# Moving the sums of w_out and the storing of its tiles in a fused retention and feed-forward kernel

## The chip, the cores and the metric

The kernel runs on one core of one Trainium2 chip. The metric is the device time of one execution in microseconds (us); the time of a kernel is the median of its runs.

## What is computed

Eight batches, eight heads, 576 positions, head dimension 64: retention (attention without softmax, with a decay per head), then a feed-forward layer of 512 -> 2048 -> 512 with g = h - tanh(h).

```python
scores = scale * np.matmul(q, k.transpose(0, 1, 3, 2))
ret = scores * Dmat[None]                    # Dmat: gamma_h ** (i - j) for i >= j, else 0
attn = np.matmul(ret, v)
x = attn.transpose(0, 2, 1, 3).reshape(4608, 512)
h = x @ w_in                                 # 512 x 2048
g = h - np.tanh(h)
out = g @ w_out                              # 2048 x 512
```

## The kernel before

**Work and its order.** The 576 positions are cut into nine chunks n = 0 to 8 of 64 positions, so a chunk holds 512 tokens (8 batches x 64). The 2048 hidden features are cut into sixteen F tiles f of 128. Each matmul operand in float32 is held as two words, high ("hi", `gh`, `xh`) and low ("lo", `gl`, `xl`), and a product is made of high x high, high x low and low x high. The program order is kept on each engine (`in_order`); a DMA may further be put behind a named instruction (`behind`). Nearly all DMAs go through one queue, that of SyncE (SP), in the order in which they stand in the program: a DMA that waits for its data holds all behind it.

**Chunks 0 and 1** come first. **Chunk 2** is then done in two halves. In the first, the loop over f calls `mm1(2, f)` (h of one F tile, tanh on ScalarE (ACT) at L533, the difference on VectorE (DVE) at L534, a store to DRAM) and, on VectorE, two pieces of the sums of w_in (`summed`). In the second, `stage_b(2, 0)`, the F tiles run in pairs: at an even f `attend(m)` makes one *turn* of the retention for later chunks (a turn is two batches of one chunk: scores, outputs, state), and each f has `mm2(2, f)`, twelve matmuls into the output's four PSUM banks. Here `split` makes the two words of g two tiles ahead (ACT copy, then VectorE), `fetch` loads g four tiles ahead, and `load_turn` loads q and k (t = 0) or v and k (t = 1) of later turns. The load of v for turn m+2 is put behind the seventh matmul of the odd F tile's `mm2`. `scale_v` (L301), four ACT instructions, multiplies v of a turn with its table, one turn ahead, inside `attend`. The fifth and sixth matmul of the odd tile's `mm2` wait for the loads of q of turn m+2 and of v of turn m+1.

**Keeping w_out.** The last six chunks use a scheme with seven products for a pair of 2 x 2 blocks in place of eight, for which sums of the weight blocks are needed. `keep_whole` adds the two words of one F tile of w_out on VectorE (L1021) and stores the result to `owhole` in DRAM (L1022). Before the change it does so for tiles 0 to 7 at the odd f of the first half, into the buffers with tag "cv" (four, which the activations of `mm1` also use), and for tiles 8 to 15 at the odd f of the second half, into two quarters of `work`.

**Chunks 3 to 8** are taken in pairs: `stage_c(na, ...)` for na = 3, 5 and 7. Each has eight *steps* p, one for a pair of F tiles. A step (for na = 3 and 5) begins with a stretch of the retention for a later turn (`attend_c`: 64 x 64 matmuls at L344, which include those that read the scaled v), and then has seven products `product_c` numbered 0 to 6, six matmuls each (L1078). Between them stand the VectorE sums `u2` (L1202), `u4` (L1210), `c22` (L1218), `c12` (L1225), `g11` (L1241), `c21` (L1247); ACT's tanh (L1183); GpSimd's (POOL's) difference for `c22`, `c12` and `c21` (L1187); and four spills to DRAM through SP (L1140), each two products after it was made. In odd steps VectorE also makes the four sums `sums_of` (L1117 to L1120). `prep_turn(m0 + p + 1, 1)` after product 5 is the scaling of v (L301) that the next step's stretch needs.

**The sums of w_out** are spread over the sixteen steps of na = 3 and 5, numbered `step_` 0 to 15, two for each pair j of F tiles: `load_whole(j)` (L1027) loads two tiles from `owhole` to `work`, `out_sums` makes four VectorE subtractions of 128 x 256 (L1035), `out_words` is one ACT copy to the high words (L1040), `out_lows` one VectorE subtraction for the low words (L1044), and `store_sums` stores to `osum` and `ovar` (L1048, L1049). The next load goes to the buffer that the store reads. Before the change, the even step has `out_sums` after product 4, `out_words` after the tanh of product 5 and ahead of the scaling of v, `out_lows` after product 6; the odd step has `store_sums` after product 0 and the next `load_whole` after product 4. `load_raws` and `load_sums` (L1062, L1070) load the weights' words for the products, the latter two steps ahead.

After na = 7, whose steps have no retention, a last part (`second_product`, L1399 and L1403) makes the second layer of chunks 3 to 8 with seven products in the same way.

Of the kernel before, what the change touches and what calls it, by code (L numbers as in the profile page):

```python
# [9 lines left out]
F32 = mybir.dt.float32  # L10
# [82 lines left out]
def retention_ffn(ctx: ExitStack, tc: tile.TileContext, ins, out, spill, wvar, owhole, osum, ovar):  # L93
# [924 lines left out]
    def keep_whole(f, r):  # L1018

        w = wout[f].bitcast(F32)  # L1020
        nc.vector.tensor_tensor(r, w[:, 0], w[:, 1], op=ALU.add)  # L1021
        nc.sync.dma_start(owhole[:, f], r)  # L1022

    def load_whole(j):

        if j < NPAIR:
            nc.sync.dma_start(work[:, 0:2], owhole[:, 2 * j : 2 * j + 2])  # L1027
# [18 lines left out]
    def store_sums(j):  # L1046

        nc.sync.dma_start(osum[:, :, j], work[:, 3].rearrange("p (v m) -> p v m", v=2))  # L1048
        nc.sync.dma_start(ovar[:, :, j], work[:, 0:2])  # L1049
# [94 lines left out]
    def stage_c(na, m0, lows):  # L1144

        nb, last_ = na + 1, na + 2 == NC
        if not last_:
            first_sources(na)
        for p in range(NPAIR):
            if p == 1 and not last_:  # L1150
                new_sources(na)
            back = (na - LATE) // 2 % 2 == 1
            j = NPAIR - 1 - p if back else p
            homes_ = (("o0", "own")[p % 2], "new", "h", "h") if last_ else (("o0", "h")[p % 2], "o1", "o2", "o3")
            step_ = None if last_ else NPAIR * (na - LATE) // 2 + p
            sums_of = None if last_ else attend_c(m0 + p)
            if sums_of and p == NPAIR - 1:
                sums_of()
                sums_of = None
            u2, u4 = [pool.tile([P, BLK], F32, tag=t, name=f"u{t}{na}_{j}") for t in ("gh", "gl")]  # L1160
            x, y, z, v = [
                psp.tile([P, BLK], F32, tag=t, bufs=2 if t == "h" else 1, name=f"p{w}{na}_{j}")
                for w, t in zip("xyzv", homes_)
            ]
            f1, f2 = 2 * j, 2 * j + 1
            c22, c12 = [pool.tile([P, BLK], F32, tag="g", bufs=3, name=f"c{t}_{na}_{j}") for t in (22, 12)]
            c21 = pool.tile([P, BLK], F32, tag="gl", name=f"c21_{na}_{j}")

            def done(k):
                made_at[0] += 1  # L1170
                if last_:
                    ahead_c(p, k)
                elif p == NPAIR - 1 and k < 6:
                    lows.insert(0 if k == 5 else len(lows), renew(na, k))
                spill_made(2)

            def low():
                if lows:
                    lows.pop(0)()

            def tanh(c):
                th = pool.tile([P, BLK], F32, tag="cv", bufs=4, name=f"th{na}_{j}")
                nc.scalar.activation(th, c, AF.Tanh)  # L1183
                return th

            def away(n, c, f):
                nc.gpsimd.tensor_tensor(c, c, tanh(c), op=ALU.subtract)  # L1187
                to_spill.append((made_at[0], n, f, c))

            product_c(na, j, 0, x)  # L1190
            nc.scalar.copy(u2, x)
            if na > LATE and p == 0:
                lows.append(renew(na - 2, 6))
            done(0)
            if not last_:
                load_turn(m0 + p + 3, 0)
            if step_ == 0:
                load_whole(0)
            if step_ is not None and step_ % 2:
                store_sums(step_ // 2)  # L1200
            product_c(na, j, 1, y)
            nc.vector.tensor_tensor(u2, y, u2, op=ALU.add)  # L1202
            low()
            done(1)
            if not last_:
                load_turn(m0 + p + 2, 1)
                if na == LATE:
                    load_raws(6 + p)
            product_c(na, j, 2, z)
            nc.vector.tensor_tensor(u4, z, u2, op=ALU.add)  # L1210
            if not last_:
                prep_turn(m0 + p + 2, 0)
            if sums_of:
                sums_of()
            low()
            done(2)
            product_c(na, j, 3, v)
            nc.vector.tensor_tensor(c22, v, u4, op=ALU.add)  # L1218
            low()
            done(3)  # L1220
            y = psp.tile([P, BLK], F32, tag=homes_[1], bufs=1, name=f"pw{na}_{j}")
            product_c(na, j, 4, y)
            load_sums(na, j - 2 if back else j + 2)
            away(nb, c22, f2)
            nc.vector.tensor_tensor(c12, y, u4, op=ALU.add)  # L1225
            done(4)
            if tables and not last_:
                load_tables(tables.pop())
                set_tables()
            if step_ is not None and step_ % 2:  # L1230
                load_whole(step_ // 2 + 1)
            if step_ is not None and step_ % 2 == 0:
                words = out_sums(step_ // 2)
            product_c(na, j, 5, x, False)
            if not last_ and p == NPAIR - 1:
                low()
            away(nb, c12, f1)
            g11 = tanh(x)
            if step_ is not None and step_ % 2 == 0:
                out_words(words)  # L1240
            nc.vector.tensor_tensor(g11, x, g11, op=ALU.subtract)  # L1241
            to_spill.append((made_at[0], na, f1, g11))
            if not last_:
                prep_turn(m0 + p + 1, 1)
            done(5)
            product_c(na, j, 6, v, False)
            nc.vector.tensor_tensor(c21, v, u2, op=ALU.add)  # L1247
            away(na, c21, f2)
            low()
            if step_ is not None and step_ % 2 == 0:  # L1250
                out_lows(words)
            done(6)
        spill_made(0)

# [186 lines left out]
    def fetch_on(n, f):  # L1441
        if f < NF:
            fetch(n, f)

    def stage_b(n, m0):

        fetch(n, 3)
        for f in range(NF):
            def ahead():
                if f + 2 < NF:  # L1450
                    split(n, f + 2, fetched.pop((n, f + 2)), f % 3 == 0)

            if n == 2 and f == 1:
                load_tables(FIRST)
            m, odd = m0 + f // 2, f % 2 == 1
            if n < NC - 1 and not odd:
                attend(m, ahead)
            else:
                ahead()
            if n == NC - 1:  # L1460
                fetch_on(n, f + 4)
            if n == LATE - 1:
                if odd:
                    keep_whole(8 + f // 2, work[:, f // 2 % 2])
                if f in (11, 13):
                    load_sums(LATE, (f - 11) // 2)
                if f > 3 and f % 2 == 0:
                    load_raws(f // 2 - 2)
            if (n, f) != (NC - 1, NF - 2):
                seen = [came.get((m + 2, 0)), came.get((m + 1, 1))] if n < NC - 1 and odd else []  # L1470
                names = mm2(n, f, [a for a in seen if a])
            if n < NC - 1:
                if n != LATE - 3 or (m + 3 - odd, odd) not in ((held, True), (held + 1, True)):
                    load_turn(m + 3 - odd, int(odd), names[6 if odd else 2])
                fetch_on(n, f + 4)
            if odd and tables:
                load_tables(tables.pop())
                set_tables()
            if n == 2 and f == 2:
                set_tables()  # L1480


    for f in range(NF):
        mm1(2, f, seen=[here[24, 1], came[1, 0]] if f == NF - 1 else [])
        if f == 0:
            mm2(*late[-1])
        if f == 1:
            follow(1)
        for _ in range(2):
            next(summed, None)  # L1490
        if f == 2:
            load_turn(2, 0)
        if f == 6:
            prep_turn(2, 0)
            load_turn(1, 0)
            load_turn(1, 1)
        if f in (9, 10):
            prep_turn(1, f - 9)
        if 10 < f < 14:
            fetch(2, f - 11)  # L1500
        if f > 13:
            split(2, f - 14, fetched.pop((2, f - 14)), False)
        if f % 2:
            keep_whole(f // 2, pool.tile([P, DM], F32, tag="cv", bufs=4, name=f"whole{f // 2}"))
    assert next(summed, 0) == 0
    work = pool.tile([P, 4, DM], F32, tag="xl1", bufs=1, name="work")
    stage_b(2, 0)
    lows = []
    for n in range(LATE, NC, 2):
        stage_c(n, 8 * (n - FIRST) // 2 + 8 if n < NC - 2 else None, lows)  # L1510
# [84 lines left out]
```

## Time and profile before

| | |
|---|---|
| Time, median of 3 runs | 886.43 us (886.01 to 888.31) |
| The profiled execution: time, span | 883.95 us, 882.1 us |
| TensorE matmul (PE) | 835.8 us busy, 95% |
| VectorE (DVE) | 642.0 us, 73% |
| ScalarE (ACT) | 425.7 us, 48% |
| GpSimd (POOL) | 109.7 us, 12% |
| DMA | 207.27 MB, mean 235 GB/s |

The span is the time from the first to the last instruction of the profiled execution; the time stands 1.85 us above it. PE is TensorE's matmul row, PEld its weight loads, which overlap with it, SP the DMA queue. In a table of stretches the columns are: length, busy time and number of instructions for PE, PEld, DVE, ACT and POOL, the clock that TensorE was granted (1.00 is full), the busy share of the 16 DMA engines, and GB/s. In a list of waits the columns are the engine and line that stood idle, what it waited for, the total in us, how many times, and the longest. In a timeline they are start and duration in us, engine, line, operation, and in brackets the engine's idle time before it and what ended it. In a line's own view durations are in ns, minimum/median/maximum.

### The profile page before, as it was taken

What the parts mean: (1) busy time and instruction counts of PE and PEld (TensorE: products, weight loads), DVE (VectorE), ACT (ScalarE), POOL (GpSimd) and SP (SyncE); (2) the same over time, 40 slices, a digit from 0 to 9 for tenths busy, and PEclk for the clock granted to TensorE, in tenths of its full rate; (3) what the DMA queues carried; (4) which work ended last, traced back from release to release, by engine and by line L of the source; (5) the groups of instructions that cost most, each with busy time, mean ns of one, the idle gap of its engine ahead of it and who ended that gap; (6) DMA issues with size and microseconds to landing.
All of it is one profiled execution on the core that took longest, in us unless ns stands there. A gap on an engine that the chain in (4) does not pass through costs nothing. (4 is left out here: it accounts for less than half of the span.)

```text
span 882.1 us, 19386 instructions
## 1 busy us (share of the span) xinstructions
PE 835.8 (95%) x7893; PEld 696.5 (79%) x7894; DVE 642.0 (73%) x950; ACT 425.7 (48%) x767; POOL 109.7 (12%) x87
## 2 busy tenths in 40 slices
PE   8999999999998986999888999999999999999997
PEld 6788888878877765877776777888788888888886
DVE  6998877776776745566694556756789888888884
ACT  4987755443343433242453243643555544445442
POOL 0000101020000001231332132343320000000000
PEclk9999999999999989999998899999999999999999
DMA  9968968884887878998677685489795445444311
GB/s 344 362 220 291 329 221 253 258 281 138 270 318 264 273 283 273 334 308 312 233 256 256 214 285 184 144 315 322 272 388 169 132 140 153 126 140 147 120 25 48
DMA packets 101768, 207.27 MB, mean 235 GB/s; under 512 B 9136, under 2 KB 42288, under 8 KB 99120
## 3 DMA queue, kind: packets, MB, share of 16 engines
q1 hardware_dynamic: 101232, 205.25, 68.5%
q8 instruction: 62, 1.02, 0.5%
q10 hardware_dynamic: 448, 0.79, 0.2%
q14 instruction: 26, 0.21, 0.1%
HBM read 134.17 MB, written 71.83 MB: 234 GB/s over the span
## 5 line engine op out<-in xcount | busy, mean ns | idle before, releaser
L1399 PE MATMUL b<-w,s 128*128 128x512 f32 x504 | 176.1, 397 | 1.0 <-ACT u L1413 0.7
L1187 POOL TENSOR_TENSOR c<-c,th 128x512 f32<-128x512 f32 x72 | 97.0, 1353 | 335.5 <-ACT th L1183 286.2
L1403 PE MATMUL b<-w,s 128*128 128x256 f32 x504 | 130.6, 280 | 0.0
L1399 PEld LDWEIGHTS b<-w,s 128*128 128x128 f32 x504 | 91.8, 188 | 18.8 <-ACT u L1413 1.0
L1183 ACT ACTIVATE th<-c 128x512 f32<-128x512 f32 x72 | 45.1, 630 | 117.4 <-DVE c L1218 92.0
L1403 PEld LDWEIGHTS b<-w,s 128*128 128x128 f32 x504 | 95.2, 189 | 5.5
L514 PE MATMUL h<-xh,wi 128*128 128x512 f32 x380 | 97.0, 392 | 1.6 <-DVE g L534 0.9
L572 PE MATMUL o<-wo,gh 128*128 128x512 f32 x344 | 89.7, 397 | 6.8 <-DMA vr<-in_qkv_dram 5.9
L344 PE MATMUL own<-qk,vr 64*64 64x64 f32 x888 | 64.2, 242 | 22.4 <-ACT vr L301 19.9
L514 PEld LDWEIGHTS h<-xh,wi 128*128 128x128 f32 x380 | 70.6, 188 | 17.0 <-DVE g L534 1.3
L572 PEld LDWEIGHTS o<-wo,gh 128*128 128x128 f32 x344 | 63.7, 189 | 23.0 <-DMA vr<-in_qkv_dram 7.2
L344 PEld LDWEIGHTS own<-qk,vr 64*64 64x64 f32 x888 | 50.2, 151 | 23.7 <-ACT vr L301 21.2
L1078 PE MATMUL px<-xhv,raw 128*128 128x512 f32 x192 | 65.0, 422 | 0.0
L344 PE MATMUL own<-qk,state 64*64 64x64 f32 x888 | 63.9, 238 | 0.0
L1202 DVE TENSOR_TENSOR ugh<-py,ugh 128x512 f32<-128x512 f32 x24 | 16.6, 692 | 53.9 <-PE py L1078 48.1
L514 PE MATMUL h<-xl,wi 128*128 128x512 f32 x192 | 51.8, 390 | 0.0
L572 PE MATMUL o<-wo,gl 128*128 128x512 f32 x172 | 48.5, 396 | 1.2 <-DMA vr<-in_qkv_dram 1.2
L344 PEld LDWEIGHTS own<-qk,state 64*64 64x64 f32 x888 | 49.6, 150 | 0.0
L1413 ACT COPY u<-b 128x512 f32<-128x512 f32 x36 | 21.1, 586 | 52.4 <-PE b L1399 52.4
L1362 DVE TENSOR_TENSOR s<-sums,s 128x1024 fp32r<-128x1024 f32 x36 | 43.8, 1232 | 2.1 <-ACT s L1358 2.1
L1358 ACT CAST s<-sums 128x1024 fp32r<-128x1024 f32 x36 | 37.9, 1053 | 13.1 <-DVE sums L1360 9.7
L1078 PEld LDWEIGHTS px<-xhv,raw 128*128 128x128 f32 x192 | 37.0, 201 | 8.2
(317 smaller groups left out, 1882.9 us busy)
## 6 DMA issues: line engine op xcount, KB each, us to landing
wt<-wvar_dram SPq DMA_DIRECT2D x20, 1024.0 KB, 5.4
spill_dram<-c SPq DMA_DIRECT2D x72, 256.0 KB, 4.4
qk<-in_qkv_dram SPq DMA_DIRECT2D x29, 512.0 KB, 5.6
vr<-in_qkv_dram SPq DMA_DIRECT2D x29, 512.0 KB, 5.9
ge<-spill_dram SPq DMA_DIRECT2D x12, 1024.0 KB, 5.8
go<-spill_dram SPq DMA_DIRECT2D x12, 1024.0 KB, 5.1
s<-spill_dram SPq DMA_DIRECT2D x46, 256.0 KB, 4.2
spill_dram<-g SPq DMA_DIRECT2D x36, 256.0 KB, 3.7
```

The source lines that it names most:

```text
L344: nc.tensor.matmul(out_, w, x, start=start, stop=stop)
L514: nc.tensor.matmul(hp, win[f][:, cc // 2, a, cc % 2 * P : (cc % 2 + 1) * P], x[:, cc, :], start=(k == 0), stop=(k == 3 * NCC - 1))
L572: nc.tensor.matmul(ops[n][t], g[:, t * P : (t + 1) * P], wout[f_][:, a, :], start=(f_ == first and k == 0), stop=(f_ == final and k == 2),)
L1078: nc.tensor.matmul(into, w[:, a, k], x[:, k], start=start and i == 0, stop=i == len(terms) - 1, skip_group_check=not start,)
L1183: nc.scalar.activation(th, c, AF.Tanh)
L1187: nc.gpsimd.tensor_tensor(c, c, tanh(c), op=ALU.subtract)
L1202: nc.vector.tensor_tensor(u2, y, u2, op=ALU.add)
L1358: nc.scalar.copy(hi, src)
L1362: nc.vector.tensor_tensor(lo, src, hi.bitcast(F32), op=ALU.subtract)
L1399: nc.tensor.matmul(to, hi[:, j], ws, start=fresh and j == 0, stop=last_, skip_group_check=not fresh)
L1403: nc.tensor.matmul(to[:, 0], lo[:, j], ws[:, 0], start=False, stop=False, skip_group_check=not fresh)
L1413: nc.scalar.copy(t, to)
```

## The change

In the first half of chunk 2 the sums of tiles 0 to 7 go to the buffers "gh" and "gl" in turn, at f = 1, 3, 5, 7, 9, 11, 12 and 13. The store of a kept tile is issued by a new function, `store_whole`, in the next F tile, behind that tile's own loads; in the second half the sum itself stands after `mm2` and the loads. In the steps, `out_sums` moves from after product 4 of the even step to its end; `out_words` and `out_lows` move to the odd step, after products 2 and 3; `store_sums` moves from after product 0 to after product 5 of the odd step; and `load_whole` from after product 4 of the odd step to after product 1 of the next even step. No arithmetic is added or left out.

```diff
@@ keep_whole
         w = wout[f].bitcast(F32)
         nc.vector.tensor_tensor(r, w[:, 0], w[:, 1], op=ALU.add)
-        nc.sync.dma_start(owhole[:, f], r)
+        to_keep.append((f, r))
+
+    to_keep = []
+
+    def store_whole():
+
+        while to_keep:
+            f, r = to_keep.pop()
+            nc.sync.dma_start(owhole[:, f], r)
@@ stage_c, a step
             done(0)
             if not last_:
                 load_turn(m0 + p + 3, 0)
-            if step_ == 0:
-                load_whole(0)
-            if step_ is not None and step_ % 2:
-                store_sums(step_ // 2)
             product_c(na, j, 1, y)
...
                 if na == LATE:
                     load_raws(6 + p)
+                if step_ % 2 == 0:
+                    load_whole(step_ // 2)
             product_c(na, j, 2, z)
...
             done(2)
+            if step_ is not None and step_ % 2:
+                out_words(words)
             product_c(na, j, 3, v)
             nc.vector.tensor_tensor(c22, v, u4, op=ALU.add)
             low()
+            if step_ is not None and step_ % 2:
+                out_lows(words)
             done(3)
...
-            if step_ is not None and step_ % 2:
-                load_whole(step_ // 2 + 1)
-            if step_ is not None and step_ % 2 == 0:
-                words = out_sums(step_ // 2)
             product_c(na, j, 5, x, False)
...
             g11 = tanh(x)
-            if step_ is not None and step_ % 2 == 0:
-                out_words(words)
             nc.vector.tensor_tensor(g11, x, g11, op=ALU.subtract)
...
             done(5)
+            if step_ is not None and step_ % 2:
+                store_sums(step_ // 2)
             product_c(na, j, 6, v, False)
...
             low()
             if step_ is not None and step_ % 2 == 0:
-                out_lows(words)
+                words = out_sums(step_ // 2)
             done(6)
@@ stage_b
             if n == LATE - 1:
-                if odd:
-                    keep_whole(8 + f // 2, work[:, f // 2 % 2])
...
                 fetch_on(n, f + 4)
+                store_whole()
+                if odd:
+                    keep_whole(8 + f // 2, work[:, f // 2 % 2])
@@ first half of chunk 2
+    KEEP = (1, 3, 5, 7, 9, 11, 12, 13)
...
-        if f % 2:
-            keep_whole(f // 2, pool.tile([P, DM], F32, tag="cv", bufs=4, name=f"whole{f // 2}"))
+        store_whole()
+        if f in KEEP:
+            at = KEEP.index(f)
+            keep_whole(at, pool.tile([P, DM], F32, tag=("gh", "gl")[at % 2], name=f"whole{at}"))
...
     stage_b(2, 0)
+    store_whole()
```

## The prediction

> **What bounds the kernel now.** I read the page, the busy time by stretch, the waits, then the timeline of single steps. First the three stretches that the change touches: the last fifteen F tiles' first products of chunk 2 with their sums, chunk 2's second half (eight pairs of F tiles), and the sixteen steps with `step_` 0 to 15. Columns: length, busy us by engine, granted clock, DMA share, GB/s.
>
> ```profile
> 217.25:259.35 42.10, 41.20 (x182) 33.54 (x180) 30.62 (x55) 13.98 (x27) 0.00 (x0) 1.00 0.84 287
> 259.35:333.73 74.38, 65.92 (x1218) 52.66 (x1217) 44.83 (x91) 31.20 (x81) 0.00 (x0) 0.95 0.79 281
> 333.73:563.10 229.37, 203.93 (x2560) 168.76 (x2560) 145.05 (x233) 91.20 (x196) 60.42 (x46) 0.93 0.74 256
> ```
>
> TensorE (PE, first number) is the bound, but idle for 0.90, 8.46 and 25.44 us here, and below full clock in the last two. The waits of PE, ACT and the DMA queue (SP), which follow, say for whom.
>
> ```profile
> PE own L344 <- ACT vr L301: 19.9, 9, 5.5
> PE o L572 <- DMA vr<-in_qkv_dram: 8.5, 6, 3.4
> ```
> ```profile
> ACT work L1040 <- DVE work L1035: 19.7, 8, 5.6
> ACT vr L301 <- DMA vr<-in_qkv_dram: 19.3, 7, 5.8
> ```
> ```profile
> SPq L1022 <- DVE work L1021: 42.4, 8, 7.1
> ```
>
> So PE waits nine times for ACT's scaling of v (`scale_v`, L301), which stands behind `out_words` (L1040), which waits for `out_sums` (L1035) on VectorE; and six times for a load of v that SP issues late, since SP is held for 42.4 of 74 us by the store in `keep_whole` (L1022).
>
> **Chunk 2's second half.** SP around the worst pair, and ACT at the landing:
>
> ```profile
> 312.97 0.32 SPq L1022 DMA_DIRECT2D owhole_dram<-work  x1
> 313.35 1.06 SPq L1070 DMA_DIRECT2D wt<-wvar_dram  x1
> 314.50 0.38 SPq L895 DMA_DIRECT2D vr<-in_qkv_dram  x1
> ```
> ```profile
> 320.12 1.28 ACT L301 ACTIVATE vr<-vr,vtab 128x128 f32<-128x128 f32 x4 [5.75 <-DMA vr<-in_qkv_dram]
> ```
>
> It is a ring: the load of v for turn m+2 stands behind the store of w_out's words on SP; that store waits for VectorE's sum, which in VectorE's order follows `split`'s low words; these wait for ACT's copy, which follows the scaling of v of turn m+1, which waits for its own load. Each load thus starts only after the one before has landed and been worked on. The change stores a tile after the next F tile's loads, so its sum is done and SP isn't held. What then holds the load of v is its own wait for the seventh matmul of the odd F tile (`late`), which leaves five matmuls of the pair to run, and PE needs it a pair later. A pair costs
>
> ```profile
> 285.41:293.10 7.69, 7.69 (x154) 6.39 (x153) 6.06 (x13) 4.16 (x12) 0.00 (x0) 1.00 0.83 277
> 310.53:323.42 12.89, 9.46 (x153) 7.22 (x152) 5.48 (x12) 4.01 (x11) 0.00 (x0) 0.83 0.85 317
> ```
>
> 7.69 us where nothing is late. 8 x 7.69 = 61.5, so at most 12.9 us go. In the pairs of F tiles 11 and 13 the 1 MB load of L1070 still stands just ahead of the load of v (1.06 us of issue), for which I leave 0.8 each, an estimate between 0 and 1.5: **-11.3**. VectorE's order of the sums is unchanged (only the last moves behind two output copies). The eight stores are as many as before, each landing beside PE's work.
>
> **The first stretch.** Sums now write buffers of their own ("gh", "gl") instead of the four "cv" buffers that the activations use.
>
> ```profile
> ACT g L533 <- DMA owhole_dram<-whole: 4.3, 1, 4.3
> ```
>
> ACT stood 4.3 us for such a buffer; PE's idle 0.90 us is the end of that. Three sums now fall in F tiles 11 to 13, one per tile, 0.7 us more on a VectorE that is busy 30.6 of 42.1: covered. **-0.9** (0 to -0.9).
>
> **The steps.** Steps 0, 1, 2, 3 by PE's starts (even, odd, even, odd), then steps 6, 8 and 10:
>
> ```profile
> 333.73:345.50 11.77, 11.77 (x172) 9.77 (x171) 7.63 (x14) 4.28 (x9) 2.47 (x2) 1.00 0.67 182
> 345.50:365.43 19.93, 14.45 (x172) 12.04 (x171) 9.54 (x19) 5.44 (x13) 2.56 (x3) 0.83 0.98 343
> 365.43:377.44 12.01, 12.01 (x172) 9.99 (x171) 7.73 (x11) 4.67 (x11) 5.00 (x5) 1.00 0.94 333
> 377.44:393.09 15.65, 13.76 (x172) 11.44 (x171) 9.22 (x18) 5.43 (x13) 2.69 (x3) 0.89 0.88 296
> 420.65:433.93 13.28, 12.18 (x172) 9.99 (x171) 7.74 (x11) 4.67 (x11) 5.02 (x5) 1.00 0.76 269
> 448.08:461.33 13.25, 12.28 (x172) 10.13 (x171) 12.16 (x17) 7.66 (x15) 5.26 (x4) 1.00 0.64 224
> 477.81:494.11 16.30, 13.90 (x171) 11.31 (x170) 8.18 (x13) 4.68 (x11) 5.00 (x5) 0.90 0.66 227
> ```
>
> The same work takes 12.0 us in an even step and 15.65 in the odd one. The end of step 2, on VectorE, ACT and PE:
>
> ```profile
> 375.49 3.28 DVE L1035 TENSOR_TENSOR work<-work 128x256 f32<-128x256 f32 x4
> ```
> ```profile
> 376.25 0.60 ACT L1183 ACTIVATE th<-px 128x512 f32<-128x512 f32 x1
> 378.80 0.62 ACT L1040 CAST work<-work 128x512 fp32r<-128x512 f32 x1 [1.96 <-DVE work L1035]
> 379.33 0.40 ACT L301 ACTIVATE vr<-vr,vtab 128x128 f32<-128x128 f32 x1
> ```
> ```profile
> 379.77 0.27 PE L344 MATMUL own<-qk,vr 64*64 64x64 f32 x2 [1.89 <-ACT vr L301]
> ```
>
> With `out_words` gone from here, L301 starts at 376.8 instead of 379.33, its first part is done at 377.2, ahead of PE's need at 377.88 (379.77 less the 1.89). The gap of 1.89 us goes, and so does what follows it:
>
> ```profile
> 380.53:383.94 3.41, 3.41 (x88) 3.10 (x84) 1.42 (x3) 1.24 (x4) 1.27 (x1) 0.50 0.56 202
> ```
>
> 3.41 us at half clock, 1.7 us lost. An odd step becomes 11.8 us (step 0's length, no gap).
>
> What is added elsewhere: in the odd step `out_words` (0.62 us) stands on ACT after product 2, when ACT has nothing to do until the first tanh: free. `out_lows` stands between `c22` and `c12` on VectorE.
>
> ```profile
> L1044 DVE TENSOR_TENSOR work<-work x8: 678/682/683, 351.5 to 551.1; 128x512 fp32r<-128x512 f32 x8
> ```
> ```profile
> 365.16 1.26 ACT L301 ACTIVATE vr<-vr,vtab 128x128 f32<-128x128 f32 x4
> ```
>
> In step 1, L301 at 365.16 was just in time for the next stretch at 365.43. The 0.68 us delays `c12`, so tanh, so L301, by up to 0.68: I take 0.5 at each odd step's end. Even 12.5 and odd 11.8: 12.15 on average.
>
> The new `out_sums` stands at the end of the even step on VectorE, with the next step's mask product, state sum and `u2` queued behind it. It now waits for a load issued only five products earlier. Where PE's first product and SP's loads stand in step 2 (start 365.43), and the landings of the load and of the store that frees its buffer:
>
> ```profile
> 367.67 0.73 PE L1078 MATMUL px<-xhv,raw 128*128 128x512 f32 x2
> ```
> ```profile
> 370.71 0.37 SPq L895 DMA_DIRECT2D vr<-in_qkv_dram  x1
> 371.42 0.80 SPq L1062 DMA_DIRECT2D raw<-wvar_dram  x2
> ```
> ```profile
> L1027 SPq DMA_DIRECT2D work<-owhole_dram x8: 332/382/422, 342.8 to 534.4; - x8
> ...
> DMA to landing us min/median/max: 3.5/6.7/8.6
> ```
> ```profile
> L1049 SPq DMA_DIRECT2D ovar_dram<-work x8: 569/570/591, 356.4 to 554.7; - x8
> ...
> DMA to landing us min/median/max: 3.2/5.6/6.8
> ```
>
> Counted from the even step's start: the stores go out near +1.6 (after the spill of `c22`, two issues), land near +7.2; the load goes out behind vr and raw near +7.4 and lands at +14.1, while VectorE is ready at +12.7. It stands 1.4 us and ends the sums at about +16. The mask product and state sum are not needed before the next stretch, and `u2`'s second term comes at about +17 (12 + a stretch of 2.24 + two products of 1.40, the seven taking 9.77 of step 2), so this is hidden up to a landing at +14.6; each us later goes to PE about one for one. I take nothing. On SP the two stores go ahead of the spills of `c12` and `c21`, whose GpSimd work is later still, and the load goes ahead of L1070 and may hold it about 1 us for the landing of the stores; PE uses what L1070 loads two steps later: nothing. Step 0 is the same with SP behind eight output stores: the load lands near +16, 1.0 us.
>
> A rule bears on the place: the Trainium skill, SBUF — State Buffer, section "SBUF: two separate sides", says that a VectorE operation with two SBUF inputs and a GpSimd operation lock each other out for the whole instruction. The trace agrees where L1035 took 3.28 us beside GpSimd's `c12`; by it the moved sums meet `c21` instead, about 1 us more, hidden as above.
>
> ```profile
> PE own L344 <- issue: 2.4, 1, 2.4
> ```
>
> Of the 229.37 us: 16 x 12.15 = 194.4; kept are step 10's excess of 4.3 (its gap, in this row, waits for nothing that the profile shows), 1.3 in step 6 and 1.25 in step 8, before which ACT and VectorE also renew x; there `out_lows` stands behind `low` and beside GpSimd's `c22`, 1.3 more, an estimate at twice its 0.68; step 0, 1.0; and DMA: a pair with loads of raw moves 12.01 x 333 + 15.65 x 296 = 8.6 MB, which at step 1's 343 GB/s takes 25.2 us and not 24.3, so up to 0.9, taken as 0.5 for three pairs, 1.5. Sum 205.0: **-24.4**.
>
> **Sum.** 0.9 + 11.3 + 24.4 = 36.6. The profiled execution took 883.95 (span 882.1): 847.4. It lies 2.5 us under the median of 886.43: 850 for the median.
>
> **Rivals.** (1) The wait moves to VectorE: stores land at the slow end (+8.4), the load takes 8.6, lands at +17, and PE loses 2.4 us in each of eight odd steps: 18 less gain, 868. For it: DMA share 0.94 to 0.98 in steps 1 and 2; against: 0.66 in step 10. (2) DMA is the bound in the first six steps: these save nothing but step 1's own gap, some 8 less, 858. (3) The change doesn't do what it says in chunk 2: v stays late because DMA share is 0.79 already; only the steps gain, 861. (4) The clock: half-clock spells stay though gaps go, so only the idle time is won, 8.5 + 25.4 less 6.5 that is kept or new: 27, 859. The even steps at 1.00 speak against. Beside it: the Trainium skill, TensorE: Matmul & The Clock Gate, Part 1, puts the fall to half clock after an idle window of about 3.4 us, which a gap of 1.89 us isn't; the trace differs, so the measurement decides. (5) Slower: the load of w_out's tiles under `out_sums`, as in (1), but so late that each odd step loses more than 36.6 / 8 = 4.6 us, or 2.9 with a half-clock spell again: a landing past +17.5, that is over 10 us after issue where the slowest so far took 8.6; about 892.
>
> **How the numbers follow.** Forecast 0.57 (843 to 858), (1) 0.16, (2) 0.09, (3) 0.08, (4) 0.04, (5) 0.04, no change 0.02. Within 0.3% (2.7 us) is what a measurement can't tell from no change. Faster 0.94, same 0.02, slower 0.04. The low end is every step at 11.8 with the issue gaps kept and chunk 2 at 61.5: 886.4 - 0.9 - 12.9 - 33 = 839.6; the high end takes in (1), 868.
>
> **What would show it.** Right: no wait of SP for L1021; pairs of 7.7 us; PE's waits for L301 down to a few of about 0.5; odd steps near 12 at clock 1.00. Wrong: VectorE idle at L1035 behind the load for over 2 us in most even steps (rivals 1, 5); PE waiting for v in chunk 2 (3); half-clock spells without gaps (4); or PE waits for raw or wt loads, which have none now (2).

## The result, and the profile after

The changed kernel takes 844.23 us (median; 841.34 to 845.69) against 887.37 us (886.01 to 892.31): ratio 0.950, 95% interval 0.9455 to 0.9546. In a later comparison on one chip it took 845.46 against 883.08, ratio 0.958 (0.9545 to 0.9617). The forecast was 850, with a range of 839 to 868.

The line numbers move in the changed kernel: the products are L1086 (before L1078), `keep_whole`'s store L1030 (L1022), `load_whole` L1035 (L1027), `out_sums` L1043 (L1035), `out_words` L1048 (L1040), `out_lows` L1052 (L1044), `c22` L1226 (L1218), `c12` L1235 (L1225); the scaling of v stays L301. The same stretches as before, and the rest behind them (length, busy us of PE, PEld, DVE, ACT, POOL, clock, DMA share, GB/s):

```profile
216.29:257.23 40.94, 40.94 (x182) 33.52 (x180) 31.08 (x56) 14.03 (x27) 0.00 (x0) 1.00 0.86 286
257.23:323.04 65.81, 63.27 (x1217) 51.43 (x1216) 45.27 (x92) 31.54 (x82) 0.00 (x0) 0.99 0.91 323
323.04:524.25 201.21, 193.39 (x2561) 158.96 (x2561) 139.63 (x229) 90.67 (x193) 60.43 (x46) 0.99 0.80 287
524.25:843.30 319.05, 312.65 (x1681) 267.24 (x1679) 250.55 (x292) 153.03 (x209) 35.89 (x27) 1.00 0.55 181
```

The first half of chunk 2 falls from 42.10 to 40.94, its second half from 74.38 to 65.81. The sixteen steps fall from 229.80 to 201.21 (up to the first product of step 16; the forecast's table cut this 0.43 us earlier). The rest is unchanged (318.57 before). TensorE's idle time in these steps is 7.8 us instead of 25.4, and its busy time 11.0 us less (193.39 instead of 204.36) at a clock of 0.99 instead of 0.93. Its waits after:

```profile
PE own L344 <- ACT vr L301: 5.2, 7, 2.9
...
PE o L572 <- DMA vr<-in_qkv_dram: 2.3, 2, 1.8
```

19.9 and 8.5 us have become 5.2 and 2.3. The DMA queue's own waits show the other cause gone: 42.4 us at the store of a kept tile have become 2.0.

```profile
SPq L1030 <- DVE t L992: 1.0, 1, 1.0
...
SPq L1030 <- DVE qk L295: 0.6, 2, 0.4
...
SPq L1030 <- DVE t L991: 0.4, 1, 0.4
```

Steps 2, 3, 4 and 8 (they were 12.01, 15.65, 12.00 and 13.25):

```profile
348.15:361.09 12.94, 12.28 (x172) 10.12 (x171) 6.60 (x10) 6.21 (x16) 5.33 (x5) 1.00 0.97 353
361.09:372.86 11.77, 11.77 (x171) 9.76 (x170) 9.43 (x18) 4.37 (x10) 2.68 (x3) 1.00 1.02 376
372.86:385.45 12.59, 12.26 (x171) 10.12 (x170) 6.59 (x10) 5.87 (x15) 5.01 (x5) 1.00 0.92 345
423.21:439.82 16.61, 13.72 (x171) 11.43 (x170) 12.45 (x18) 7.72 (x17) 4.94 (x4) 0.90 0.68 238
```

Steps 3, 5, 11 and 13 have no idle time left; of the other odd steps, step 1 (12.57) and step 7 (13.39, with 1.01 us idle for `c22`) are the long ones. Most even steps are 0.6 longer than before. The timeline at the end of step 3 shows why, on VectorE, ACT and TensorE:

```profile
370.20 0.68 DVE L1226 TENSOR_TENSOR c<-pv,ugl 128x512 f32<-128x512 f32 x1
370.81 0.68 DVE L1052 TENSOR_TENSOR work<-work 128x512 fp32r<-128x512 f32 x1
371.40 0.68 DVE L1235 TENSOR_TENSOR c<-pw,ugl 128x512 f32<-128x512 f32 x1
```
```profile
372.72 0.58 ACT L1191 ACTIVATE th<-px 128x512 f32<-128x512 f32 x1
373.20 0.68 ACT L301 ACTIVATE vr<-vr,vtab 128x128 f32<-128x128 f32 x2
```
```profile
373.64 0.27 PE L344 MATMUL own<-qk,vr 64*64 64x64 f32 x2 [0.33 <-ACT vr L301]
```

`out_lows` stands between `c22` and `c12`; the tanh of `c12`, the tanh behind it and the scaling of v each come 0.6 us later, and the stretch waits 0.33 at first and a little for each of v's four parts after. Step 8 is the same thing in its worst form: at the end of step 7 VectorE also has the low words of the next chunks' x (L1140), and `out_lows`, now beside GpSimd's `c22`, takes 1.77 us instead of 0.68:

```profile
421.49 1.22 DVE L1140 TENSOR_TENSOR xlv<-src,xhv 128x1024 fp32r<-128x1024 f32 x1
422.62 1.77 DVE L1052 TENSOR_TENSOR work<-work 128x512 fp32r<-128x512 f32 x1
424.31 0.68 DVE L1235 TENSOR_TENSOR c<-pw,ugl 128x512 f32<-128x512 f32 x1
```
```profile
426.54 0.27 PE L344 MATMUL own<-qk,vr 64*64 64x64 f32 x2 [2.89 <-ACT vr L301]
```
```profile
427.21:430.63 3.42, 3.42 (x94) 3.13 (x87) 2.60 (x4) 2.27 (x5) 1.77 (x2) 0.50 0.55 198
```

The gap of 2.89 us brings one of the two half-clock spells that are left in this execution.

### The profile page after: what moved, and what is told of

The parts are those of the page before. It is cut to its first block, busy times and chain, and to the rows that moved or that the text cites. A ratio compares the mean times of both kernels' runs of the same rounds, so it can differ in the third digit from the quotient of the medians.

```text
span 843.3 us, 19373 instructions
## 1 busy us (share of the span) xinstructions
PE 821.8 (97%) x7893; PEld 684.2 (81%) x7894; DVE 640.6 (76%) x950; ACT 425.3 (50%) x767; POOL 109.9 (13%) x87
## 4 chain that ended last, share of the span: by engine, by line
PE 46%; DVE 2%; issue 1%; ACT 1%; DVEq 0%; ACTq 0%
PE b L1405 18%; PE b L1409 9%; PE px L1086 4%; PE pv L1086 4%; PE pw L1086 3%; PE py L1086 2%; PE pz L1086 2%; PE own L344 1%; DVE work L1052 1%; ACT th L1191 1%; DVE xlv L1140 1%; DVE c L1235 0%; PE s L344 0%; PE new L344 0%; ACT vr L301 0%
## 5 line engine op out<-in xcount | busy, mean ns | idle before, releaser
L572 PEld LDWEIGHTS o<-wo,gh 128*128 128x128 f32 x344 | 63.5, 188 | 16.9 <-ACT gh L553 2.8
L1086 PE MATMUL px<-xhv,raw 128*128 128x512 f32 x192 | 61.5, 402 | 1.0 <-issue 1.0
L344 PE MATMUL own<-qk,vr 64*64 64x64 f32 x888 | 56.9, 226 | 5.3 <-ACT vr L301 5.2
L344 PE MATMUL own<-qk,state 64*64 64x64 f32 x888 | 57.9, 225 | 0.0
L344 PEld LDWEIGHTS own<-qk,vr 64*64 64x64 f32 x888 | 46.0, 138 | 6.4 <-ACT vr L301 6.4
L344 PEld LDWEIGHTS own<-qk,state 64*64 64x64 f32 x888 | 46.0, 138 | 0.0
L514 PEld LDWEIGHTS h<-xl,wi 128*128 128x128 f32 x192 | 36.0, 188 | 7.7
L1086 PEld LDWEIGHTS px<-xhv,raw 128*128 128x128 f32 x192 | 35.0, 189 | 8.7 <-issue 1.2
```

What stands on the lines that cost most here:

```text
L344: nc.tensor.matmul(out_, w, x, start=start, stop=stop)
L514: nc.tensor.matmul(hp, win[f][:, cc // 2, a, cc % 2 * P : (cc % 2 + 1) * P], x[:, cc, :], start=(k == 0), stop=(k == 3 * NCC - 1))
L572: nc.tensor.matmul(ops[n][t], g[:, t * P : (t + 1) * P], wout[f_][:, a, :], start=(f_ == first and k == 0), stop=(f_ == final and k == 2),)
L1086: nc.tensor.matmul(into, w[:, a, k], x[:, k], start=start and i == 0, stop=i == len(terms) - 1, skip_group_check=not start,)
```

## The experiments

**The two parts alone.** e1 has only the hunks of `keep_whole`, `stage_b` and the first half of chunk 2; e2 has only those of `stage_c`.

> The part for chunk 2 alone (buffers of their own in the first half, sum and store of a tile one F tile later in the second), the steps as before. Theory (two separate causes that add up): chunk 2's second half takes 66 us instead of 74.4 and the first half about 1 less, the sixteen steps stay at 229 to 230: about 10 us less than before, 877. Rival (the two parts need one another, since the steps only gain if the kept tiles come earlier or the other way round): under 3 us less, or over 20.

> The part for the steps alone (sums at the end of the even step, words in the middle of the odd one, load and stores moved with them), chunk 2 as before. Theory: the sixteen steps take 201 us instead of 229.8, chunk 2's second half stays at 74: about 28 us less than before, 858. Rival (parts need one another): clearly less than 28, with the rest only seen when both are in.

e1 took 872.25 against 885.43 (ratio 0.9866, 0.9812 to 0.992), e2 858.23 (0.9715, 0.9664 to 0.9767). Second half of chunk 2 and steps, first in e1, then in e2:

```profile
256.60:319.52 62.92, 62.26 (x1217) 50.95 (x1216) 44.57 (x90) 30.86 (x81) 0.00 (x0) 1.00 0.96 337
319.52:552.94 233.42, 206.38 (x2561) 170.85 (x2561) 145.52 (x233) 91.66 (x197) 60.82 (x46) 0.92 0.73 251
```
```profile
258.80:333.32 74.52, 66.15 (x1217) 52.73 (x1216) 45.01 (x91) 31.40 (x81) 0.00 (x0) 0.95 0.80 282
333.32:535.19 201.87, 192.96 (x2561) 158.43 (x2561) 138.76 (x231) 91.38 (x195) 60.71 (x46) 0.99 0.80 287
```

Each part moves its own stretch and leaves the other near where it was: the second half takes 74.5 us in e2 against 74.4 before, the steps 233.4 in e1 against 229.8 (2.6 of the 3.6 in step 10, whose gap of unknown cause was 4.42 us there instead of 2.40). 13.2 and 27.2 add up to 40.4, and both together gave 37.6 to 43.1: two separate causes.

**Only the store later.** The sum stays ahead of `mm2`, the first half keeps its "cv" buffers, and the DMA alone is put off:

```diff
@@ keep_whole: tiles 8 to 15 are stored later, 0 to 7 at once
-        nc.sync.dma_start(owhole[:, f], r)
+        to_keep.append((f, r))
+        if f < 8:
+            store_whole()
@@ stage_b
                 fetch_on(n, f + 4)
+                if not odd:
+                    store_whole()
```

> The kernel before with one thing changed: in chunk 2's second half the store of a kept tile is issued behind the next F tile's loads. The sum stays where it was, the first half and the steps too. Theory (the DMA queue of SyncE is held by the store, so v's loads come late): the second half falls from 74.4 to about 66 us, 8 us less, 878. Rival (the place of the sum or the shared buffers count): within 2 us of before.

873.39 against 885.43 (0.9889, 0.9822 to 0.9956; like e1 a gain of little over 1%, but with an interval that ends below 1), and the second half takes 62.5 us. Its last two pairs, the worst before with 12.89 and 10.31:

```profile
305.97:314.01 8.04, 7.76 (x154) 6.38 (x153) 3.54 (x7) 3.44 (x9) 0.00 (x0) 1.00 1.02 391
314.01:322.34 8.33, 8.11 (x152) 6.40 (x152) 6.17 (x14) 3.40 (x11) 0.00 (x0) 1.00 0.98 383
```

So the place of the store in the DMA queue is the whole of the second half's gain; moving the sum and giving it buffers of its own add at most the microsecond of the first half.

**Only the copy later.** Of the steps' moves one is made, and within the same even step:

```diff
             g11 = tanh(x)
-            if step_ is not None and step_ % 2 == 0:
-                out_words(words)
             nc.vector.tensor_tensor(g11, x, g11, op=ALU.subtract)
...
                 prep_turn(m0 + p + 1, 1)
+            if step_ is not None and step_ % 2 == 0:
+                out_words(words)
             done(5)
```

> The kernel before with one line moved: the ACT copy out_words stands behind the scaling of v in the same even step, instead of ahead of it. The four sums stay where they were and stay slow beside GpSimd. Theory (PE waits since ACT's queue has the scaling of v behind the copy): the gaps of 1.9 us and the half-clock spells go, odd steps fall from 15.3 - 15.7 to about 12, steps 2 to 15 save some 20 us and step 0 and 1 some 5: about 25 us less, 861. Rival (the late sums on VectorE are what counts, through the difference g11 and c21 that stand behind them): odd steps stay above 14 us, under 8 us less, 880 or more.

857.32 against 885.43 (0.971, 0.9655 to 0.9765): as much as e2. VectorE and ACT at the end of its step 2, and its steps 5 and 6:

```profile
370.97 2.63 DVE L1035 TENSOR_TENSOR work<-work 128x256 f32<-128x256 f32 x4
```
```profile
372.16 1.27 ACT L301 ACTIVATE vr<-vr,vtab 128x128 f32<-128x128 f32 x4
373.63 0.62 ACT L1040 CAST work<-work 128x512 fp32r<-128x512 f32 x1 [0.20 <-DVE work L1035]
```
```profile
398.64:410.41 11.77, 11.77 (x171) 9.76 (x171) 9.03 (x18) 4.81 (x11) 2.71 (x3) 1.00 0.86 301
410.41:422.42 12.01, 12.01 (x171) 9.98 (x170) 7.73 (x11) 5.26 (x14) 5.02 (x5) 1.00 1.02 378
```

The sums are still slow beside GpSimd, `out_words` still waits for them, but the scaling of v no longer stands behind it, and the steps shown are short, the even one shorter than the 12.6 of the changed kernel. (Steps 4 and 10 took 14.21 and 16.11 us here, each with a gap of about 2 us that waits for nothing the profile shows.) The slow sums cost nothing that shows by themselves; what cost was that ACT's queue put work that TensorE needed behind a copy that nobody needed soon.

**The chunk 2 part with only the copy moved.** e1 and e3 together.

> The kernel before with the change's part for chunk 2 and, of the steps, only the copy out_words moved behind the scaling of v; sums, low words, load and stores of w_out in the steps stay where they were. Theory (in the steps the place of that one copy in ACT's queue was the whole cost): about 41 us less than before and, as even steps keep 12.0 us with nothing added ahead of c12, some 3 to 5 less than the changed kernel, 840. Rival (the moves of sums and load are worth something beside it): slower than the changed kernel, 848 or more.

841.08 against 882.66 (0.9535, 0.9505 to 0.9566). Its steps 4 and 5:

```profile
372.00:384.01 12.01, 12.01 (x171) 9.98 (x170) 7.73 (x11) 5.26 (x14) 5.02 (x5) 1.00 1.03 400
384.01:395.79 11.78, 11.78 (x172) 9.77 (x171) 9.05 (x18) 4.81 (x11) 2.73 (x3) 1.00 0.99 349
```

Steps 2, 4 and 6 take 12.0 to 12.3 us. Seen against the changed kernel's 844 to 845, of other comparisons, it is no slower; by the intervals the two can't be told apart. So the other moves in the steps show no gain beside the copy's.

**`out_lows` behind `c12`.**

```diff
             low()
-            if step_ is not None and step_ % 2:
-                out_lows(words)
             done(3)
...
             nc.vector.tensor_tensor(c12, y, u4, op=ALU.add)
+            if step_ is not None and step_ % 2:
+                out_lows(words)
             done(4)
```

> The changed kernel with out_lows behind c12 instead of ahead of it in the odd step. Theory (out_lows delays c12, so tanh, so the scaling of v that the next even step's stretch needs): steps 2 to 14 with even numbers fall from 12.6 to 12.0 us, and the wait of 2.9 us at the start of step 8 by 1 to 2: about 5.5 us less than the changed kernel, 839. Rival (even steps are longer for another reason, for instance VectorE's sums at their end or DMA load): even steps stay at 12.6, same time, 844.

839.23 against 882.66 (0.9515, 0.9483 to 0.9547). Steps 4 and 5:

```profile
370.31:382.30 11.99, 11.99 (x171) 9.98 (x170) 6.46 (x10) 5.27 (x14) 5.25 (x5) 1.00 0.98 359
382.30:394.14 11.84, 11.84 (x172) 9.69 (x171) 8.73 (x18) 4.61 (x10) 2.37 (x3) 1.00 1.03 372
```

Steps 2, 4 and 6 take 12.0 to 12.3 again, the gap at step 8 falls from 2.89 to 1.20, and no half-clock spell is left in the steps. Beside the changed kernel on one chip:

> The changed kernel as it is, timed beside the next two on one chip: 843 to 846.

> The changed kernel with out_lows behind c12, as before, now beside the changed kernel on one chip. Theory: 5 to 6 us less than it, 839. Rival (the difference seen lay in the chips of the two jobs): within 2 us of it.

840.50 (838.87 to 842.05) against 845.46 (844.75 to 847.58): 5.0 us, with ranges that don't touch. By the medians this is the fastest version that was run; e8's range (839.95 to 843.98) overlaps with that of e5 beside it (838.16 to 841.31).

**A later load.** `load_whole` after product 4 of the even step instead of product 1:

```diff
-                if step_ % 2 == 0:
-                    load_whole(step_ // 2)
             product_c(na, j, 2, z)
...
             done(4)
+            if step_ is not None and step_ % 2 == 0:
+                load_whole(step_ // 2)
```

> The changed kernel with load_whole after product 4 of the even step instead of product 1, so the load lands some 2 to 2.5 us later, near +16.5 us from the even step's start. Theory (a late landing is hidden up to +14.6 or so and then goes to TensorE about one for one, since VectorE stands at out_sums): 1.5 to 2 us lost in each pair of steps, 12 to 17 in all, 859; up to 872 if gaps bring half-clock spells back. Rival (VectorE's reserve in the odd step hides it): within 3 us of the changed kernel.

856.75 against 882.66 (0.9712, 0.9674 to 0.9751), some 12 us over the changed kernel (e6, which differs from it in where one load is issued, took 844.81 in the same comparison). Waits of TensorE and of VectorE (`u2` is L1206 here); the sums after step 4, which starts at 378.30; and step 5:

```profile
PE pw L1086 <- DVE ugh L1206: 8.7, 6, 5.0
```
```profile
DVE work L1043 <- DMA work<-owhole_dram: 29.4, 6, 8.5
```
```profile
397.09 1.68 DVE L1043 TENSOR_TENSOR work<-work 128x256 f32<-128x256 f32 x4 [5.06 <-DMA work<-owhole_dram]
```
```profile
391.23:405.67 14.44, 12.37 (x172) 9.62 (x171) 8.74 (x18) 4.03 (x9) 2.36 (x3) 1.00 0.88 320
```

Rival (1) made real: VectorE stands 5.06 us at the sums, a product waits for `u2` behind them, and the odd step takes 14.44 instead of 11.78. The load landed at +18.8 and cost 2.7 us, so here the cost begins near +16. But that even step took 12.93 us; step 2 of e7 took 11.77, its load landed at +17.7, step 3 took 14.63, and there the cost begins near +14.9. Counted from the odd step's own start, both put the point near +3.1, which is +15.1 for an even step of 12.0 us. In the changed kernel's profiled execution the landing is at +14.2 after step 4's start:

```profile
380.79 0.58 SPq L1035 DMA_DIRECT2D work<-owhole_dram  x1
```
```profile
387.06 1.55 DVE L1043 TENSOR_TENSOR work<-work 128x256 f32<-128x256 f32 x1 [0.81 <-DMA work<-owhole_dram]
```

In its other profiled execution (f1) the store of step 3's sums took 8.4 us to land, the load of step 4 waited for it on SP and then took 8.1 us itself, and rival (1) came true in this pair of steps. VectorE after step 4, which starts at 372.17, and step 5:

```profile
389.98 1.68 DVE L1043 TENSOR_TENSOR work<-work 128x256 f32<-128x256 f32 x4 [4.41 <-DMA work<-owhole_dram]
```
```profile
384.76:398.57 13.81, 12.38 (x171) 9.61 (x170) 8.74 (x18) 4.05 (x9) 2.37 (x3) 1.00 0.97 346
```

The price past that point is one for one. In steps 1, 3 and 5 of the executions with the sums at the end of the even step, ten loads landed 4.0 to 6.2 us after the odd step's start with no half-clock spell in it, and each of these odd steps took the landing plus 8.6 to 8.7 us; all that landed before +3.1 left it at 11.8.

**The weight sums behind v's load** in the pairs of F tiles 11 and 13: `load_sums` is moved from ahead of `mm2` to behind `store_whole()`.

> The changed kernel with the 1 MB load of weight sums at F tiles 11 and 13 of chunk 2 issued behind v's load instead of ahead of it. Theory (v's load is late in the last two pairs since it stands behind that 1 MB): these two pairs fall from 19.4 us to 16 to 17, 2 to 3 us less, 842. Rival (the DMA engines are busy at a share near 1 there, so the order doesn't matter): under 1 us, 844.

844.81 against 882.66 (0.9575, 0.9543 to 0.9606): nothing. The last two pairs in the changed kernel, and in this one:

```profile
303.62:312.41 8.79, 8.07 (x154) 6.31 (x153) 3.55 (x7) 3.44 (x9) 0.00 (x0) 1.00 1.02 366
312.41:323.04 10.63, 8.81 (x152) 6.73 (x152) 6.87 (x16) 3.96 (x11) 0.00 (x0) 0.92 0.73 290
```
```profile
303.44:312.07 8.63, 7.77 (x154) 6.39 (x153) 3.55 (x7) 3.45 (x9) 0.00 (x0) 1.00 1.01 362
312.07:319.85 7.78, 7.78 (x152) 6.48 (x152) 6.93 (x16) 3.87 (x11) 0.00 (x0) 1.00 0.98 380
```

The pairs look 3 us shorter, but the changed kernel's own second execution (f1) had 9.03 and 8.02, so it is within what executions differ by; the time agrees. With the DMA engines busy at a share near 1.0, another transfer was the late one in this execution: v's load was in time, and q's product with its table (L295), which stood 5.1 us for the load of the table, came 0.86 late.

**The last tile first.** To the kernel with `out_lows` behind `c12`, the last kept tile's sum and store ahead of the last `mm2` and its eight output stores:

```diff
+                if f == NF - 1:
+                    keep_whole(8 + f // 2, work[:, f // 2 % 2])
+                    store_whole()
                 if f in (11, 13):
...
-                if odd:
+                if odd and f < NF - 1:
                     keep_whole(8 + f // 2, work[:, f // 2 % 2])
```

> The kernel with out_lows behind c12, and beside it the sum and store of the last kept tile ahead of the last F tile's second products, so that the store goes ahead of the eight output stores and the load of step 0, which waits for it, goes out some 2 us earlier. Theory (steps 0 and 1 are 2 us too long since that load lands late and VectorE stands at out_sums): step 1 falls from 13.8 to about 12.2, 837.5. Rival (the output stores, now later, or the sum ahead of the output copies cost as much): 839.

841.48 (839.28 to 842.58), not faster than 840.50. The load goes out 10.9 us after step 0's start instead of 12.1, but it takes 6.8 us to land instead of 5.1, so it lands no earlier (+17.6, and +17.2 in f2) and step 1 is no shorter (14.45, and 14.09). v's load for step 1 is late now too:

```profile
335.27 0.27 PE L344 MATMUL own<-qk,vr 64*64 64x64 f32 x2 [0.70 <-ACT vr L301]
```

## Why the prediction was right

By its own terms, each against the profiled executions:

- **First half, -0.9:** measured -1.2. Right.
- **Second half, -11.3:** -8.6 in the profiled execution of the changed kernel, and -9.8 to -12.0 (62.4 to 64.6 us) in the nine other profiled executions whose store comes late. The mechanism, a ring through the DMA queue, is shown by e4. The spread lies mostly in the last two pairs (16.1 to 19.4 us), where several loads are in flight at a DMA share near 1; which of them is late differs by execution. The -8.6 holds a gap of 1.82 us and a half-clock spell behind it, which none of the nine others has.
- **The steps, -24.4:** measured -28.6. The even and odd steps were forecast at 12.5 and 11.8; most even ones came at 12.6, odd ones at 11.8 and, from step 11 on, 11.0 to 11.3. The landing at +14.1 came at +14.2 to +15.0 in steps 2, 4 and 6. What was mis-sized is the list of what was kept: step 10 kept 1.2 of its 4.3 us (13.69), as its gap was 1.0 us instead of 2.4 and no half-clock spell followed; step 6 kept none of its 1.3; and the 1.5 for DMA was hardly paid, since a pair with loads of raw took 24.4 to 24.7 us at 345 to 376 GB/s where I had capped the rate at step 1's 343 (the profile before has 354 in its step 4). The other way, step 7 took 13.39 instead of 11.8, and step 8, by the sum's terms 15.05 (12.5 + 1.25 + 1.3), took 16.61: three subtractions of low words stood ahead of `out_lows`, which took 1.77 us. Its idle time of 2.89 us is about the 3.05 allowed over 12.0; what the sum left out is the half-clock spell behind it, 1.7 us.
- **The hiding of the load up to +14.6** was too strict by about 0.5 us for the even step of 12.0 us that it was worked out with (+15.1), and the point moves out with the even step's length. One for one past it was right.
- **What the change's moves are worth one by one** the prediction didn't ask. It costed the new places of the sums, low words, load and stores at almost nothing and the copy's old place at nearly all, and e3 bears that out: one copy moved behind the scaling of v gives the whole gain of the steps, and all the other moves together show no gain beside it (e8), while `out_lows` in its new place costs 0.6 us of each even step (e5).
- **Rivals.** (2) fell: steps 1 to 5 move 345 to 398 GB/s and TensorE waits for none of their loads of raw or weights. (3) fell with e4, (4) with the clock of 0.99 in the steps. (1) is real as a mechanism: e7 shows it, and f1 pays 2.0 us in step 5. In both executions of the changed kernel the landings of the other steps but step 0 were in time, so it was not the rule. Step 0's load landed at +16.5 and +16.9, for which step 1 pays 0.8 and 1.9 us (the forecast had 1.0). Losses as large as (5) needs came only in e7, whose load of step 0 landed at +21.0.

Some of the closeness is luck: in the profiled executions chunk 2's second half gained 2.7 us less than forecast and the steps 4.2 more, and these two errors nearly cancel in the total of 38.3 us against 36.6.

On the clock: before, nine half-clock spells lay in the three stretches, two of them double; after, there are two, one behind a gap of 1.82 us and one behind 2.89. The forecast followed the row, not the rule of an idle window of 3.4 us in the Trainium skill (TensorE: Matmul & The Clock Gate, Part 1), and the runs agree with the row.

Left open: the gap near step 10 that waits for nothing the profile shows. It was 2.4 us before, 1.0 in the changed kernel, and 0.8 to 4.4 in the others, at much the same place in the program; no run here tells what it is.

## What to carry to other kernels

Where a chain of waits runs through an engine's or a DMA queue's order, ask which single instruction in that queue is early for what it is needed for, and move that one: here one ACT copy (28 us) and one kind of store (12 us), each behind the next work that the bound engine needs, make up the whole gain by their sum (the two alone were not run together). Moving a whole group of work instead also moves its other instructions to places where they may delay something, as the low words ahead of `c12` did (5 us). A load whose consumer stands in front of other work on an in-order engine has a latest landing that can be worked out from the timeline; be on the safe side of it, since here each microsecond past it cost one, and DMA landings differ by execution (f1).

## What the hardware showed that I had not expected

An idle gap of 1.8 to 1.9 us was often, not always, followed by 3.41 us at half clock; gaps up to 1.64 us never were, and in e8 one of 3.01 us was not, so the gap's place in time counts beside its length. The traces show how. In each execution all spells start on one grid of 3.41 us (before: 380.52, 407.83 and 465.86, that is 8 and then 17 grid windows apart). Count TensorE's idle time in each window of that grid that ran at full clock, from 40 to 820 us in the thirteen kept traces: all 35 windows with 1.88 us or more were followed by half clock, none of the 34 with 1.0 to 1.7 us was, and of four with 1.80 to 1.86 two were. The 3.01 us of e8 fell as 1.64 and 1.37 on two windows.

The DMA engines carried 376 GB/s (step 3 after) and 400 (step 4 of e8) through whole steps of 12 us with loads and stores mixed, above the 343 that I had taken for a limit, and the median landing of `load_whole` did not rise (5.8 us after, 6.7 before). And a VectorE subtraction of 128 x 256 that takes 0.42 us took up to 1.55 beside one GpSimd instruction of 1.28 us in its new place, and up to 1.48 in its old one.
